# Stores of the weight forms' high parts issued by ScalarE instead of SyncE, in a fused attention and two-MLP kernel

## The chip, the cores and the metric

The kernel runs as one program on one core of a Trainium2 chip. The metric is the device time of one execution in microseconds (us). Engines are named as in the profile: PE (TensorE), DVE (VectorE), ACT (ScalarE), POOL (GpSimd) and SP (SyncE, which here does nothing but issue transfers).

## What is computed

Attention over 4 x 8 heads of 576 positions with a mask by blocks of 64, then two MLPs without bias on the 2304 rows that come out of it, all in 32-bit floats:

```python
scores = scale * np.matmul(q, k.transpose(0, 1, 3, 2))
scores = np.where(mask, scores, -1000000000.0)
attn = np.exp(scores - np.max(scores, axis=-1, keepdims=True))
attn = attn / (np.sum(attn, axis=-1, keepdims=True) + 1e-09)
x = np.matmul(attn, v)              # 2304 x 512 after the heads are joined
h = x @ w_in                        # 512 -> 2048
x = (h * np.clip(h + 3.0, 0.0, 6.0) / 6.0) @ w_out
h = x @ w2_in
out = (h * np.tanh(softplus(h))) @ w2_out
```

## The kernel before

**Matmuls in three products.** Each 32-bit operand is kept as a high and a low part (`wh`, `wl`; `Xh`, `Xl`; `gh`, `gl`); a product is high x high, high x low and low x high (`products`, L840 to L847). A high part is an ACT copy that rounds (`copy`, L313, recorded at L316), the low part a subtraction on DVE or POOL (`sub`, L320, recorded at L322).

**Stages.** Attention runs to about 165 us. The first MLP follows in three blocks of tokens (512, 256, 512): for each of 16 slices of the inner dimension `in1` makes `h` in one of two PSUM banks (12 matmuls), ACT computes `e` = relu(h + 3), DVE multiplies (`multiply`, L950), ACT copies `gh`, DVE subtracts `gl`, and two slices later `out1` multiplies with them (12 matmuls). The last 1024 tokens (`in3`, `out3`, from 388 us) and the whole second MLP (from about 535 us) take block products in seven forms instead of eight. That needs sums of blocks of the weights:

- `unit1(q)`, L1232 to L1273, eight times: sums of blocks of the first `w_out`, high and low parts stored to the DRAM tensor `w1d`;
- `unit2(u)`, L1004 to L1046, sixteen times: two raw tiles of 512 KB are loaded (L1012), rebased from 64-bit floats by ACT, POOL and DVE (`rebase`, L849), four block sums `S` formed, and for four pieces the high part is copied by ACT (`hx`, `Sh`; L1043) and stored (L1044), the low part subtracted (`q`, `ex`; L1045) and stored (L1046), all to `w2d`. All units use the same tiles, so a piece can be written again only when its store has landed, and a raw tile loaded again only when it was read.

The units run beside the matmuls, from about 237 us (`unit1`) and 287 us (`unit2`) to 533 us. `weights1` and `weights2` load the forms back.

**Order.** Nothing is ordered by hand there. `Schedule` (L123 to L248) takes every operation with its engine, a cost and, for transfers, a time to land, plays the whole program once, and issues each engine's list in the order of the start times that come out. TensorE's operations are bound to the order of the program; the others are chosen by how soon TensorE needs what follows from them. A transfer is an operation of SP whose cost grows with its size, so SP's list is the planner's picture of all DMA:

```python
"POOL": (145, 2.156), "POOL_ONE": (100, 0.99), "POOL_V": (260, 0.87), "SP": (100, 3.05),
```

(first number fixed, second per KB for SP: 880 for 256 KB, in the planner's units). At run time each engine takes its list strictly in order.

Of the kernel before, what the change touches and what calls it, by code (L numbers as in the profile page):

```python
# [55 lines left out]
LANDS = 6000  # L56
# [41 lines left out]
class Ref:  # L98
# [14 lines left out]
    @staticmethod  # L113
    def real(*views):
        def one(x):
            if isinstance(x, Ref):
                return x.get()
            return [one(y) for y in x] if isinstance(x, (list, tuple)) else x

        return [one(x) for x in views]  # L120
# [130 lines left out]
def f32(ap):  # L251
    return ap.bitcast(F32)
# [7 lines left out]
def fused_kernel(ctx: ExitStack, tc: tile.TileContext, qT, kT, vv, w1, w2, outT):  # L260
    nc = tc.nc
# [18 lines left out]
    w1d = dpool.tile([NQ, 2, P, 1792], F32, tag="w1d", name="w1d")  # L280
    w2d = dpool.tile([NQ, 2, 2, P, 1792], F32, tag="w2d", name="w2d")
# [18 lines left out]
    plan = Schedule()  # L300
    real = Ref.real
# [4 lines left out]
    def dma(kb, reads, writes, dst, src, **kw):  # L306
        def run(e):
            d, s = real(dst, src)
            nc.sync.dma_start(d, s)

        return plan.add(one("SP", "SP", kb), reads, writes, run, land=kw.pop("land", 2500), **kw)

    def copy(n, reads, writes, dst, src, func=AF.Copy, psum=False, after=(), **kw):  # L313
        def run(e):
            d, s = real(dst, src)
            nc.scalar.activation(d, s, func, **kw)  # L316

        return plan.add(one("ACT", "ACT_PSUM" if psum else "ACT", n), reads, writes, run, after=after)

    def sub(engines, reads, writes, dst, a, b, **kw):  # L320
        return plan.add(
            engines, reads, writes, lambda e: ENG[e].tensor_sub(*real(dst, a, b)), **kw)  # L322
# [78 lines left out]
    def load_v(p):  # L401
        dma(90, [], [("v", p % 2)], at["v", p % 2], vv[p], land=LAND, behind=tuple(begun[-4:]))
# [346 lines left out]
    for n in range(2):  # L749
        for j in range(2):  # L750
            r, c = slice(64 * j, 64 * j + 64), slice(64 - 64 * j, P - 64 * j)
# [16 lines left out]
    for g in range(NG + LAG_V + NU):  # L768
        p, i = divmod(g, NU)
        if g < NG:  # L770
# [7 lines left out]
            if g in EARLY_ROUNDS:  # L778
                f, c = divmod(EARLY_ROUNDS.index(g), 2)
# [3 lines left out]
        u, i = divmod(g - LAG_R, NU)  # L783
        if i == 0 and 0 <= u < NP:
            sums(u)
        u, i = divmod(g - LAG_V, NU)
# [187 lines left out]
    def before(n):  # L974
        return [*plan.readers.get(n, ()), *[x for x in [plan.writer.get(n)] if x is not None]]
# [28 lines left out]
    def unit2(u):  # L1004

        q, c = u // 2, u % 2
        at = [("r", 0), ("val", 1)]
        vs = [buf[x] for x in at]
        dst = w2d[q, c].rearrange("t p (s c) -> t p s c", c=256)
        for i in range(2):  # L1010
            raw = buf["raw", i]
            dma(512, [], [("raw", i)], raw.rearrange("p n t -> p (n t)"),  # L1012
                w2[2 * q + i, :, 512 * c:512 * c + 512].bitcast(U32), after=odd if u == 0 else (), land=LANDW)
            rebase(
                raw, buf["r", i], buf["val", i], (("raw", i), ("r", i), ("val", i), ("val", i)),
                buf["val", i] if i else None)
        cc, ch = buf["S"], buf["Sh"]
        a11, a12, a21, a22 = vs[0][:, 0:256], vs[0][:, 256:512], vs[1][:, 0:256], vs[1][:, 256:512]
        psum = lambda n: one("DVE", "DVE_PSUM", n)

        pool = lambda n: one("POOL", "POOL", n)

        def sums(n, a, b, reads, of, add=False):
            plan.add(
                of, reads, [("S", n)],
                lambda e: (ENG[e].tensor_add if add else ENG[e].tensor_sub)(*real(cc[:, n], a, b)))

        sums(0, a21, a22, [at[1]], pool(256), True)
        sums(3, a11, a21, at, psum(256))
        sums(1, cc[:, 0], a11, [at[0], ("S", 0)], psum(256))  # L1030
        sums(2, a12, cc[:, 1], [at[0], ("S", 1)], psum(256))
        view = lambda t: t.rearrange("p (s c) -> p s c", c=256)
        lo = [view(buf["q", n]) for n in range(2)]
        parts = (
            (512, view(buf["hx", 0]), view(vs[0]), ("hx", 0), [at[0]], slice(0, 2), lo[0], [("q", 0)]),
            (256, view(buf["hx", 1][:, 0:256])[:, 0:1], view(vs[1])[:, 1:2], ("hx", 1), [at[1]], slice(6, 7),
             lo[1][:, 0:1], [("q", 1)]),
            (512, ch[:, 0:2], cc[:, 0:2], ("Sh", 0), [("S", 0), ("S", 1)], slice(2, 4), view(buf["ex", 0]), [("ex", 0)]),
            (512, ch[:, 2:4], cc[:, 2:4], ("Sh", 1), [("S", 2), ("S", 3)], slice(4, 6), view(buf["ex", 1]), [("ex", 1)]),
        )  # L1040
        for i, (n, x, v, xn, vn, cs, to, tn) in enumerate(parts):
            of = (either(n) if i > 1 else pool(n)) if i else psum(n)
            copy(n, vn, [xn], x.bitcast(F32R), v, psum=not i)  # L1043
            dma(n // 2, [xn], [("w2d", q, c, 0, i)], dst[0][:, cs], x, land=LANDS if u < 2 else 2500)  # L1044
            sub(of, vn + [xn], tn, to.bitcast(F32R), v, x)  # L1045
            dma(n // 2, tn, [("w2d", q, c, 1, i)], dst[1][:, cs], to, land=LANDS if u < 2 else 2500)  # L1046

# [184 lines left out]
    def unit1(q):  # L1232

        f, g = 2 * q, 2 * q + 1
        names = lambda f: [("wt", f, 1, h) for h in range(2)]
        for h in range(2):
            dma(128, [("wt", f, 1, h)], [("w1d", q, h, 0)], w1d[q, h, :, 0:256], f32(half_b(f, h)[:, 0:256]))
            dma(256, [("wt", g, 1, h)], [("w1d", q, h, 3)], w1d[q, h, :, 1280:1792], f32(half_b(g, h)))
        m = q % 2
        v, u, vn, un = buf["val", m], buf["r", m], ("val", m), ("r", m)  # L1240
        a11, a12, a21, a22 = u[:, 0:256], u[:, 256:512], v[:, 0:256], v[:, 256:512]
        cc, ch = [raw_f32(i).rearrange("p (s c) -> p s c", c=256) for i in range(2)] if m else [buf["S"], buf["Sh"]]
        S, Sh = [("S", m, i) if m else ("S", i) for i in range(4)], [("Sh", m, i) if m else ("Sh", i) for i in range(2)]
        first = len(plan.ops)
        old = [k for i in range(2) for k in plan.readers.get(("raw", i), ())] if q == 1 else []

        def add(engines, reads, writes, dst, a, b, after=()):
            plan.add(
                engines, reads, writes, lambda e: ENG[e].tensor_add(*real(dst, a, b)), after=[*old, *after])

        psum, pool = one("DVE", "DVE_PSUM", 256), one("POOL", "POOL", 256)
        for i, x in enumerate((f, g)):
            cs, hl = slice(256 * i, 256 * i + 256), [f32(half_b(x, h)) for h in range(2)]
            ui, vi = un + (i,), vn + (i,)
            copy(256, names(x), [ui], u[:, cs], hl[0][:, 0:256], after=before(un))
            add(psum, names(x) + [ui], [ui], u[:, cs], u[:, cs], hl[1][:, 0:256])
            add(pool, names(x), [vi], v[:, cs], hl[0][:, 256:512], hl[1][:, 256:512], before(vn))
        un, vn = [un, un + (0,), un + (1,)], [vn, vn + (0,), vn + (1,)]
        add(pool, vn, [S[0]], cc[:, 0], a21, a22)
        sub(psum, un + vn, [S[3]], cc[:, 3], a11, a21, after=old)  # L1260
        sub(psum, un + [S[0]], [S[1]], cc[:, 1], cc[:, 0], a11)
        sub(psum, un + [S[1]], [S[2]], cc[:, 2], a12, cc[:, 1])
        for i in range(2):
            n, cs = [S[2 * i], S[2 * i + 1]], slice(2 * i, 2 * i + 2)
            to = [w1d[q, h, :, 256 + 512 * i:768 + 512 * i].rearrange("p (s c) -> p s c", c=256) for h in range(2)]
            copy(512, n, [Sh[i]], ch[:, cs].bitcast(F32R), cc[:, cs])
            dma(256, [Sh[i]], [("w1d", q, 0, 1 + i)], to[0], ch[:, cs])
            ln = ("ex" if m else "q", i)
            lo = buf[ln].rearrange("p (s c) -> p s c", c=256)
            sub(one("POOL", "POOL", 512), n + [Sh[i]], [ln], lo.bitcast(F32R), cc[:, cs], ch[:, cs])  # L1270
            dma(256, [ln], [("w1d", q, 1, 1 + i)], to[1], lo)
        if m:
            odd.extend(range(first, len(plan.ops)))  # L1273
# [169 lines left out]
    for kind, s, *i in sequence():  # L1443
# [50 lines left out]
        i, = i  # L1494
        q, p = s % NQ, s // NQ
# [99 lines left out]
```

## Time and profile before

| | us |
|---|---|
| median of 3 runs (lowest, highest) | 909.99 (909.47, 910.26) |
| the profiled execution | 908.69 |
| its span, first to last instruction | 906.8 |
| TensorE's matmuls | 899.3 (99%) |
| DVE, ACT, POOL busy | 699.2, 561.1, 713.5 |
| DMA queue, share of 16 engines | 76.6% |

The span is what the trace shows; the 1.9 us between it and the execution's time lie around it. All transfers run in one hardware queue, q1, begun by SP. Busy time of matmuls is modelled at their ends, and issuing a transfer does not count as busy time.

### The profile page before, as it was taken

To read this page: it belongs to the slowest core of one execution; us is meant where nothing else is said; L and a number is where in the kernel's file an instruction comes from. 1 tells how busy PE (TensorE), PEld (TensorE's weight loads), DVE (VectorE), ACT (ScalarE), POOL (GpSimd) and SP (SyncE) were. 2 spreads that over 40 slices of the span, in tenths; PEclk is the share of its full clock that TensorE was granted. 3 is DMA by queue.
4 is the path that set the end of the run, shared out by engine and by line. 5 is a ranking of instruction groups with operands and counts; after the bars stand their busy time and mean duration, and the time that the engine had idled before them with its cause. 6 is when DMAs were issued, how large, how long until landed. Compare 5 with 4: busy or idle time off the path is not lost.

```text
span 906.8 us, 16469 instructions
## 1 busy us (share of the span) xinstructions
PE 899.3 (99%) x5297; PEld 825.3 (91%) x5297; DVE 699.2 (77%) x1244; ACT 561.1 (62%) x1279; POOL 713.5 (79%) x722
## 2 busy tenths in 40 slices
PE   8999999999999999999999999999999999999998
PEld 7999999888899888878888889999999999999998
DVE  6999988888744756779999999687677666766657
ACT  7999999866754635465565666445554445545452
POOL 8998898578997535877877868788897978967775
PEclk9999999999999999999999999999999999999999
DMA  6887784496776799986987998886788867787752
GB/s 179 273 249 233 232 275 138 160 402 228 239 240 230 250 339 312 313 301 194 293 290 253 308 312 302 295 324 241 258 287 319 301 244 275 242 319 245 255 216 85
DMA packets 114918, 236.90 MB, mean 261 GB/s; under 512 B 23856, under 2 KB 37776, under 8 KB 114832
## 3 DMA queue, kind: packets, MB, share of 16 engines
q1 hardware_dynamic: 114832, 235.86, 76.6%
q8 instruction: 42, 0.69, 0.3%
q14 instruction: 44, 0.36, 0.1%
HBM read 169.87 MB, written 62.99 MB: 257 GB/s over the span
## 4 chain that ended last, share of the span: by engine, by line
PE 92%; DVE 2%; POOL 2%; DMA 2%; issue 1%; ACT 1%; SPq 0%; DVEq 0%; ACTq 0%; POOLq 0%
PE y L845 12%; PE y L846 12%; PE y L847 12%; PE h L845 10%; PE h L846 10%; PE h L847 10%; PE o L670 6%; PE t L606 5%; PE r L846 3%; PE r L847 3%; PE r L845 3%; PE s L565 3%; PE s L525 2%; DMA w2d<-ex 1%; DVE nm L507 1%
## 5 line engine op out<-in xcount | busy, mean ns | idle before, releaser
L845 PE MATMUL y<-X,wh 128*128 128x384 f32 (+1 forms) x448 | 156.0, 348 | 0.2 <-issue 0.2
L847 PE MATMUL y<-X,wl 128*128 128x384 f32 (+1 forms) x448 | 155.9, 348 | 0.0
L846 PE MATMUL y<-X,wh 128*128 128x384 f32 (+1 forms) x448 | 155.9, 348 | 0.0
L846 PE MATMUL h<-wl,wh 128*128 128x384 f32 (+1 forms) x320 | 114.0, 356 | 0.0
L847 PE MATMUL h<-wh,wl 128*128 128x384 f32 (+1 forms) x320 | 114.0, 356 | 0.0
L845 PE MATMUL h<-wh,wh 128*128 128x384 f32 (+1 forms) x312 | 111.1, 356 | 0.9 <-DVE xr L952 0.9
L322 POOL TENSOR_TENSOR X<-e,X 128x384 fp32r<-128x384 f32 (+1 forms) x90 | 99.3, 1110 | 13.3 <-ACT X L316 12.1
L1199 DVE TENSOR_TENSOR sgh<-y,sgh 128x384 f32<-128x384 f32 x129 | 70.0, 555 | 31.1 <-PE y L847 30.8
L845 PEld LDWEIGHTS y<-X,wh 128*128 128x128 f32 x448 | 84.1, 188 | 5.0 <-issue 0.5
L847 PEld LDWEIGHTS y<-X,wl 128*128 128x128 f32 x448 | 84.1, 188 | 4.3
L846 PEld LDWEIGHTS y<-X,wh 128*128 128x128 f32 x448 | 84.1, 188 | 4.2
L316 ACT ACTIVATE X<-e 128x384 fp32r<-128x384 f32 (+1 forms) x96 | 52.7, 551 | 52.2 <-POOL e L322 48.4
L322 POOL TENSOR_TENSOR X<-xr,X 128x384 fp32r<-128x384 f32 (+2 forms) x40 | 44.5, 1112 | 48.0 <-ACT X L316 40.0
L322 DVE TENSOR_TENSOR z<-t,z 128x512 fp32r<-128x512 f32 (+1 forms) x112 | 67.6, 629 | 8.9 <-ACT z L316 7.9
L845 PE MATMUL h<-X,wh 128*128 128x512 f32 (+1 forms) x192 | 68.4, 356 | 0.0
L846 PE MATMUL h<-X,wh 128*128 128x512 f32 (+1 forms) x192 | 68.0, 354 | 0.0
L847 PE MATMUL h<-X,wl 128*128 128x512 f32 (+1 forms) x192 | 68.0, 354 | 0.0
L846 PE MATMUL y<-gl,wh 128*128 128x512 f32 (+1 forms) x192 | 67.9, 354 | 0.0
L845 PE MATMUL y<-gh,wh 128*128 128x512 f32 (+1 forms) x192 | 67.9, 354 | 0.0
L847 PE MATMUL y<-gh,wl 128*128 128x512 f32 (+1 forms) x192 | 67.9, 354 | 0.0
L670 PE MATMUL o<-z,vh 128*128 128x320 f32 (+4 forms) x416 | 64.1, 291 | 0.7 <-DVE z L322 0.6
L846 PEld LDWEIGHTS h<-wl,wh 128*128 128x128 f32 x320 | 60.1, 188 | 5.1
(227 smaller groups left out, 2630.4 us busy)
## 6 DMA issues: line engine op xcount, KB each, us to landing
raw<-w SPq DMA_DIRECT2D x64, 512.0 KB
wh<-w2d SPq DMA_DIRECT2D x48, 512.0 KB
wl<-w2d SPq DMA_DIRECT2D x48, 512.0 KB
wh<-w2d SPq DMA_DIRECT2D x48, 384.0 KB
wl<-w2d SPq DMA_DIRECT2D x48, 384.0 KB
x1d<-x SPq DMA_DIRECT2D x32, 288.0 KB
w2d<-Sh SPq DMA_DIRECT2D x32, 256.0 KB
w2d<-ex SPq DMA_DIRECT2D x32, 256.0 KB
```

Source lines behind the costliest of these rows:

```text
L316: nc.scalar.activation(d, s, func, **kw)
L322: engines, reads, writes, lambda e: ENG[e].tensor_sub(*real(dst, a, b)), **kw)
L507: lambda e: nc.vector.tensor_reduce(to, view, axis=AX.X, op=ALU.max, negate=True))
L525: nc.tensor.matmul(sc[:, a:z], stationary[i][:, x, :], ks[:, y, a - o:z - o], start=k == 0 and a in (0, 512), stop=k == 2, skip_group_chec ...
L565: nc.tensor.matmul(part(h)[:, a:a + w], qs[r, x, QUERY_AT[i]:QUERY_AT[i] + P], ks[r, y, 0:w], start=False, stop=k == 2, skip_group_check=True)
L606: nc.tensor.transpose(tp[:, c, :], x, ident)
L670: nc.tensor.matmul(out, vb[:, c, h].rearrange("p t d -> p (t d)"), mov, start=k == 0, stop=k == len(todo) - 1, skip_group_check=True)
L845: nc.tensor.matmul(b, wh, xh, start=start and k == 0, stop=False, skip_group_check=True)
L846: nc.tensor.matmul(b, wh, xl, start=False, stop=False, skip_group_check=True)
L847: nc.tensor.matmul(b, wl, xh, start=False, stop=last, skip_group_check=True)
L1199: nc.vector.tensor_add(dst, src, old)
```

## The change

A new helper records a transfer as an operation of ACT with a fixed cost of 400 and a landing time of 5000, and issues it from ACT's own queue. It takes the place of `dma` for the high stores of `unit2` (all four pieces, 64 stores in all) and for the two stores of high sums in `unit1` (16 stores). The low stores stay on SP.

```diff
+    def dma_beside(reads, writes, dst, src, land=5000):
+
+        def run(e):
+            d, s = real(dst, src)
+            nc.scalar.dma_start(d, s)
+
+        return plan.add((("ACT", 400, False),), reads, writes, run, land=land)
...
             copy(n, vn, [xn], x.bitcast(F32R), v, psum=not i)
-            dma(n // 2, [xn], [("w2d", q, c, 0, i)], dst[0][:, cs], x, land=LANDS if u < 2 else 2500)
+            dma_beside([xn], [("w2d", q, c, 0, i)], dst[0][:, cs], x)
             sub(of, vn + [xn], tn, to.bitcast(F32R), v, x)
...
             copy(512, n, [Sh[i]], ch[:, cs].bitcast(F32R), cc[:, cs])
-            dma(256, [Sh[i]], [("w1d", q, 0, 1 + i)], to[0], ch[:, cs])
+            dma_beside([Sh[i]], [("w1d", q, 0, 1 + i)], to[0], ch[:, cs])
```

Since the planner plays the program anew, the lists of ACT, DVE, POOL and SP all change from about 237 us on; TensorE's list is the same. Lines behind L312 stand 8 further down in the changed kernel. Two places matter below.

ACT, around the activation of the last slice before `in3` (`e2<-h1`, the sixteenth slice of the third block). `r<-raw` begins the rebase of a raw tile, `hx` and `Sh` are high parts, `o` the results of `out1`, `wh0_12` to `wh0_14` the token tiles for `in3`, `xr1<-h0` the first activation of `in3`. Before:

```order
L316 ACTIVATE wh0_12_3083<-xr1_163 128x512
L316 ACTIVATE hx1_165<-val1_159 128x256
L316 ACTIVATE e2_2503<-h1_2498 128x512
L316 ACTIVATE hx0_162<-r0_2499 128x512
L316 ACTIVATE gh2_2506<-h1_2498 128x512
L316 ACTIVATE wh0_13_3132<-xr0_160 128x512
L316 ACTIVATE Sh_167<-S_166 128x512 x2
L316 ACTIVATE r1_2500<-raw1_158 128x512
```

And in the changed kernel:

```order
L324 ACTIVATE wh0_12_3083<-xr1_163 128x512
L324 ACTIVATE r1_2500<-raw1_158 128x512
L324 ACTIVATE e2_2503<-h1_2498 128x512
L324 ACTIVATE Sh_167<-S_166 128x512
L324 ACTIVATE gh2_2506<-h1_2498 128x512
L324 ACTIVATE Sh_167<-S_166 128x512
L317 DMA w2d_80<-Sh_167 128x512
L324 ACTIVATE r0_2499<-raw0_156 128x512
L317 DMA w2d_80<-Sh_167 128x512
L324 ACTIVATE hx1_165<-val1_159 128x256
L317 DMA w2d_80<-hx1_165 128x256
```

The copy of a raw tile now stands right ahead of `e2<-h1`. It is the ninth of `raw1`, and eight of `raw0` stand ahead of it; before, seven of each stood ahead of `e2<-h1`, and the eighth of `raw1` came behind it. Three stores follow.

SP, around the stores of the third block's results (`x2d<-o`), which follow the last `out1`. Before:

```order
L309 DMA w2d_80<-Sh_167 128x512
L309 DMA x2d_78<-o0_2684 128x512
L309 DMA x2d_78<-o1_2685 128x512
L309 DMA w2d_80<-Sh_167 128x512
L309 DMA w2d_80<-ex0_2692 128x512
L309 DMA raw1_158<-w2 128x1024
L309 DMA w2d_80<-ex1_2693 128x512
L309 DMA w2d_80<-hx1_165 128x256
```

And in the changed kernel:

```order
L309 DMA raw1_158<-w2 128x1024
L309 DMA o2_2686<-rsd_77 64x512 x2
L309 DMA w2d_80<-ex1_2693 128x512
L309 DMA raw0_156<-w2 128x1024
L309 DMA xr0_160<-x1d_76 128x512
L309 DMA w2d_80<-q0_161 128x512
L309 DMA xr1_163<-x1d_76 128x512
L309 DMA w2d_80<-q1_164 128x256
L309 DMA w2d_80<-ex0_2692 128x512
L309 DMA raw1_158<-w2 128x1024
L309 DMA w2d_80<-ex1_2693 128x512
L309 DMA x2d_78<-o0_2684 128x512
```

The stores of `hx` and `Sh` are gone from the list. The first row is the ninth load of `raw1`, the tenth stands ahead of `x2d<-o0`; before, the ninth stood behind it.

## Rows read from the trace of the kernel before

**Rows 1.** The head and first part of the page: span, busy time.
```profile
span 906.8 us, 16469 instructions
...
PE 899.3 (99%) x5297; PEld 825.3 (91%) x5297; DVE 699.2 (77%) x1244; ACT 561.1 (62%) x1279; POOL 713.5 (79%) x722
```
**Rows 2.** Waits of PE from 230 us on: us in total, times, longest.
```profile
PE h L845 <- DVE xr L952: 0.9, 1, 0.9
PE y L845 <- issue: 0.2, 1, 0.2
```
**Rows 3.** Stretches: length, each engine's busy us (instructions), granted clock, DMA share, GB/s.
```profile
core 0: us, PE busy (x) PEld busy (x) DVE busy (x) ACT busy (x) POOL busy (x), PEclk, DMA share, GB/s
260.00:280.00 20.00, 20.00 (x169) 20.00 (x168) 12.14 (x31) 11.15 (x28) 19.59 (x21) 1.00 0.74 262
287.00:300.00 13.00, 13.00 (x104) 12.66 (x103) 6.66 (x14) 5.36 (x14) 4.99 (x6) 1.00 0.54 177
320.00:340.00 20.00, 20.00 (x90) 16.58 (x89) 11.02 (x18) 8.80 (x17) 5.51 (x7) 1.00 1.00 351
300.00:388.00 88.00, 88.00 (x401) 73.36 (x400) 57.20 (x91) 45.09 (x84) 53.15 (x52) 1.00 0.94 317
440.00:460.00 20.00, 20.00 (x90) 16.55 (x89) 19.57 (x34) 12.51 (x23) 16.92 (x18) 1.00 0.89 293
```
**Rows 4.** Timeline of PE, 385 to 395 us: start, us, instruction, idle before it.
```profile
385.41 0.39 PE L845 MATMUL y<-gh,wh 128*128 128x512 f32 x1
...
385.64 0.39 PE L846 MATMUL y<-gl,wh 128*128 128x512 f32 x1
...
388.13 0.39 PE L845 MATMUL h<-wh,wh 128*128 128x512 f32 x1
...
394.61 0.50 PE L845 MATMUL h<-wh,wh 128*128 128x512 f32 x1 [0.88 <-DVE xr L952]
```
**Rows 5.** Timeline of ACT, 321 to 394 us.
```profile
321.29 0.64 ACT L316 ACTIVATE r<-raw 128x512 f32<-128x512 f32 x1 [0.30 <-DMA raw<-w]
...
380.76 0.58 ACT L316 ACTIVATE e<-h 128x512 f32<-128x512 f32 x1
...
383.97 0.60 ACT L316 ACTIVATE gh<-h 128x512 fp32r<-128x512 f32 x1
...
392.93 0.42 ACT L316 ACTIVATE hx<-val 128x256 fp32r<-128x256 f32 x1 [1.93 <-DMA w2d<-ex]
393.25 0.58 ACT L316 ACTIVATE xr<-h 128x512 f32<-128x512 f32 x1
```
**Rows 6.** Timeline of DVE, 383 to 394 us.
```profile
383.25 0.69 DVE L952 SCALAR_TENSOR_TENSOR h<-e,h 128x512 f32<-128x512 f32 x1
...
384.66 0.68 DVE L322 TENSOR_TENSOR gl<-h,gh 128x512 fp32r<-128x512 f32 x1
...
393.87 0.69 DVE L952 SCALAR_TENSOR_TENSOR xr<-xr,h 128x512 f32<-128x512 f32 x1 [1.02 <-ACT xr L316]
```
**Rows 7.** Issues of the moved stores on SP: ns shortest/median/longest, first and last start.
```profile
L309 SPq DMA_DIRECT2D w2d<-hx x32: 319/379/817, 298.3 to 527.8; - x32
...
L309 SPq DMA_DIRECT2D w2d<-Sh x32: 319/383/1047, 302.5 to 529.2; - x32
```
**Rows 8.** Issue list: count and KB each.
```profile
raw<-w SPq DMA_DIRECT2D x64, 512.0 KB
...
w2d<-Sh SPq DMA_DIRECT2D x32, 256.0 KB
```
**Rows 9.** Timeline of SP, raw loads.
```profile
287.17 0.90 SPq L309 DMA_DIRECT2D raw<-w  x2
...
297.28 0.33 SPq L309 DMA_DIRECT2D raw<-w  x1
...
314.85 0.33 SPq L309 DMA_DIRECT2D raw<-w  x1
```
**Rows 10.** Chain that ended last, 366 to 386 us: start, us, what.
```profile
369.33 7.18 DMA w2d<-ex
```

## Prediction, before the changed kernel was run

> **What bounds the kernel now.** Start with the page's first part: TensorE is busy 899.3 us of a span of 906.8 [rows 1]. The diff leaves TensorE's instructions and their order untouched, so the time can only change by the 7.5 us in which TensorE does nothing. The list of waits says where they are [rows 2]: after the attention, which the change does not reach, one wait of 0.9 us and one of 0.2 us are left; the rest lies at the start and behind the last matmul. So the change can win about 1 us. What it can lose has no such limit: any instruction of another engine that comes late enough stops TensorE, and the question is which one comes close.
>
> The table of stretches answers the next question, how full everything else is [rows 3]. From 300 to 388 us, where the first half of the weight forms is made beside the first layer's second half, DMA is 0.94 busy and moves 317 GB/s, while ScalarE works 45 of 88 us. There DMA is the scarce thing. From 440 to 460 us it is VectorE, 19.57 of 20 us.
>
> Then the place where TensorE is nearest to waiting: the change from `out1` to `in3` at 388 us. The last `out1` starts at 385.41, and its second matmul, 0.23 us later, reads `gl` [rows 4]. ScalarE's `e<-h` for it began at 380.76, `gh` at 383.97 [rows 5], VectorE's `h` at 383.25 and `gl` at 384.66 for 0.68, so `gl` was done at 385.34 [rows 6]: about 0.3 us to spare. Eight microseconds later ScalarE stood 1.93 us before an `hx` copy, so that `xr<-h` began only at 393.25; VectorE's multiplication waited for it, and TensorE stopped 0.88 us at 394.61 [rows 4 to 6]. ScalarE takes its work in order: what one copy waits for, the activation behind it waits for too.
>
> **The change, part by part.** *Issue.* 80 stores leave SP: 64 of `w2d` (32 of `hx`, 32 of `Sh`) and 16 of `w1d`. One issue took SP 0.32 to 0.38 us [rows 7], so ScalarE takes on some 80 x 0.38 = 30 us between 237 and 530 us, about a tenth of that stretch. In the stretches of rows 3 it is busy 0.41 to 0.63 of the time, and its work for TensorE waits for nothing else, so I cost this at nothing by itself; without that cover it would be 0.4 us per store that stands ahead of an activation. No row shows a store begun by ScalarE: from below the price is nothing (it would run beside the activations), from above SP's longest, 1.05 us; I take 0.38, SP's median for the same kind of transfer. The 16 `w1d` stores fall where DMA is 0.74 busy and ScalarE works 11.15 of 20 us [rows 3]: nothing.
>
> *Work given to another engine.* VectorE gets two more `ex` subtractions and GpSimd two fewer, beside single ones that change the other way. At 0.69 us each that is 1.4 us in VectorE's stretch of nearly no gaps; TensorE had no wait there, so nothing, with 1.4 us kept for the upper end.
>
> *The order of loads.* This is the large term. SP's list no longer carries the high stores, so the planner lets the raw loads and low stores move up. The bytes are the same, but more of them are now wanted earlier. Count up to the activation that the last `out1` needs, `e2<-h1` (the order above): before, ScalarE has taken seven raw tiles of each kind by then; now nine `raw1` and eight `raw0`, and the ninth `raw1` stands right ahead of `e2`. From the first raw load on, SP issues up to that ninth load 17 raw loads (8.5 MiB), 27 low stores (5.88), 12 of `x1d` (3.0), 12 of `rsd` (1.5), 16 of `w1d` (3.5), 4 of `x2d` and 2 stores to `w1d` (0.5 each): 23.38 MiB by the issue list and the order's shapes [rows 8]. ScalarE has by then issued 8 + 14 stores of 256 KB and 8 of 128 KB, 6.5 MiB. Together 29.88 MiB = 31.33 MB.
>
> When can they have moved? From 287 to 300 us DMA moved 13 x 0.177 = 2.30 MB; the first raw loads were issued at 287.17, and the next had to wait until the first were read, so I leave this as it is. From 300 us I let DMA be always busy. Its rate at full share is 317/0.94 = 337 GB/s [rows 3]. The remaining 29.03 MB need 86.1 us: the load lands at 386.1. Then `r` (0.64), `e`, `h`, `gh` and `gl` (0.58 + 0.69 + 0.60 + 0.68 and some 0.1 between them) [rows 5, 6] end at 389.4, where TensorE wants `gl` at 385.6. **TensorE waits 3.8 us.** The bounds: at 351 GB/s, the best stretch of this mix [rows 3], the load lands at 382.7 and the wait is 0.4; at the 317 actually reached it lands at 391.6 and the wait is 9.3. I take 337, the mean of the very stretch with its gaps closed, because the raw loads now stand further ahead and keep the queue filled.
>
> The same sum for the activations before it gives loads that land some 1 to 4 us behind their place, but those activations have more to spare (10.9 us from a finished `h` to its `out1`, four groups of twelve matmuls of 2.72 us as the last one's [rows 4], for a chain of 2.7), so nothing. That a landing in this stretch does take long is seen twice: a raw load issued at 314.85 held ScalarE's copy until 321.29 [rows 5, 9], and one `ex` store took 7.18 us [rows 10].
>
> *The old wait.* With TensorE 3.8 us later, the list behind `e2` (two `Sh`, three stores, `r0`, `hx1`, three `o`, two `wh`) has time to run before `in3` needs `h0` again, so the 0.9 us go.
>
> Sum: 3.8 - 0.9 = +2.9 us. Against the profiled execution, 908.69, that is 911.6; that execution lies 1.3 us below the median of the three runs, 909.99, so the forecast for a median is **912.9**. By the bounds: 0.4 - 0.9 = -0.5 gives 909.5, and 9.3 - 0.9 = +8.4 gives 918.4.
>
> From 391 us on the raw loads have room again: DMA is 0.89 busy [rows 3] and by ScalarE's list the units, now one ahead, end seven activations from `h` earlier. Nothing waits for that end.
>
> **The rivals.** *The load still comes in time (not slower).* Place: the same `r1` copy ahead of `e2`. If DMA reaches 353 GB/s from 300 us on, the ninth load lands by 382.3 and nothing waits; the 0.9 us may go as well, since the high stores no longer stand behind raw loads in SP's queue and `hx` is free sooner: 909.99 - 0.9 = 909.1. For it: 351 GB/s stood for 20 us at share 1.00 [rows 3], and a first part of the loads may move before 300 us. Against it: the stretch's own rate at full share is 337.
>
> *Only the issue moves.* What would follow if the loads were held by something else than SP's place in line, such as the buffers they fill: then they are issued when they were before, and the time stays 909.99. For it: SP waited for others' work in between, since the second pair of raw loads came 10 us behind the first [rows 9]. Against it: the new list asks for two tiles more by the same activation, and ScalarE cannot pass them. The Trainium skill ("DMA: Bandwidth & Descriptors", "Issuing engines are not separate DMA queues") says that transfers started by several engines run on the same 16 DMA engines and that starting them from several saves only the time of issue. By that rule alone the sum is zero; it also speaks against any gain in rate. That DMA is 0.94 busy from one queue agrees with it; no run here shows two queues yet.
>
> *ScalarE itself comes late (slower).* Place: 400 to 530 us, where VectorE has no gaps [rows 3] and each activation of `in3` feeds it. Some 28 stores stand there; if every third one holds an activation by 0.38 us and VectorE cannot make it up, that is 28/3 x 0.38 = 3.5 us less 0.9: 912.6. It decides when a store is issued while TensorE's bank is waiting. Against it: no wait of TensorE there before, and ScalarE works 12.51 of 20 us.
>
> **How the numbers follow.** A measurement of this kernel can tell about 0.2%, 1.8 us, from no change. Forecast 0.52, of which 0.03 fall under 1.8 us; in time 0.30; only the issue moves 0.07; ScalarE late 0.11. Slower by over 0.2%: 0.49 + 0.11 = 0.60. Within 0.2%: 0.03 + 0.27 + 0.07 = 0.37. Faster: 0.03, since TensorE has only 1.1 us of waits to give and the rest is chance between runs. The range reaches from the first rival, 909.1, to 917.5, just short of the upper bound: it leaves out about one in ten at each end. The forecast's own range is 909.5 to 918.4.
>
> **What would show it.** In the profile after: still no change in TensorE's instructions; `w2d<-Sh` and `w2d<-hx` issued by ACT for about 0.38 us; a share of DMA above 0.96 from 300 to 388 us and more GB/s than 317; ScalarE's `r<-raw` copies released by `raw<-w` by several us in sum before 390; one wait of TensorE of 2 to 5 us for `gl` or `gh` at `y` (or for `xr` at `h`) between 380 and 400 us, and the old 0.88 gone. I am wrong if TensorE has no new wait there, if the waits lie behind 400 us or have ScalarE's stores ahead of them, or if DMA's share from 300 to 388 us stays at 0.94.

## The result, and the profile after

The changed kernel takes **919.48 us** (median of 4 runs, 919.05 to 922.05), against 909.85 for the kernel before on the same chip: a ratio of 1.0106, with a 95% interval of 1.0092 to 1.012. It is 9.6 us slower. 912.9 was forecast, with 917.5 as the upper end of the range: the sign was right, the size was not.

First the head of the page after, its waits of TensorE from 230 us on (us in total, times, longest), and its stretches (length, busy us and instructions of each engine, granted clock, DMA share, GB/s):

```profile
span 917.7 us, 16477 instructions
...
PE 903.8 (98%) x5297; PEld 826.5 (90%) x5297; DVE 698.4 (76%) x1247; ACT 561.8 (61%) x1279; POOL 709.2 (77%) x719
```
```profile
PE h L853 <- DVE gl L330: 5.3, 4, 2.4
PE y L853 <- ACT gh L324: 1.2, 1, 1.2
PE h L853 <- DVE e L330: 0.7, 1, 0.7
PE h L853 <- DVE xs L960: 0.4, 1, 0.4
PE y L854 <- DVE gl L330: 0.2, 1, 0.2
PE h L853 <- DVE xr L960: 0.2, 1, 0.2
```
```profile
260.00:280.00 20.00, 20.00 (x169) 20.00 (x168) 11.28 (x30) 10.71 (x27) 18.92 (x20) 1.00 0.73 262
320.00:340.00 20.00, 20.00 (x90) 16.57 (x89) 10.44 (x18) 6.50 (x12) 5.18 (x6) 1.00 0.92 308
340.00:360.00 20.00, 14.95 (x64) 11.36 (x63) 13.44 (x23) 9.43 (x19) 5.90 (x8) 1.00 0.97 333
...
300.00:388.00 88.00, 82.71 (x372) 67.43 (x371) 58.95 (x96) 42.65 (x79) 42.73 (x44) 1.00 0.96 321
440.00:460.00 20.00, 20.00 (x90) 16.54 (x89) 19.40 (x35) 13.44 (x23) 15.56 (x16) 1.00 0.90 303
```

TensorE has as many instructions as before [rows 1] and the clock is full. The old wait for `xr` went from 0.9 to 0.2 us [rows 2]. New is a wait of 5.3 us in four pieces that has no counterpart: `in1` waits for `gl`. It lies where TensorE did not wait at all before: from 340 to 360 us it now works 14.95 of 20 us. VectorE's full stretch, 440 to 460 us, still costs nothing [rows 3].

Since TensorE's order is the same in both kernels, each of its instructions has a twin. The start of an instruction in the changed kernel less the start of its twin before, along the timeline of TensorE, says where the 10.9 us between the two spans were lost. At the time before of 170, 330, 370, 410 and 600 us the distance is 1.18, 1.18, 7.79, 10.44 and 10.86 us. So 6.6 us were lost between 330 and 370, 2.65 between 370 and 410, and 0.4 behind that. The 1.18 us arise in the attention; two profiles below in which no store moved show 1.2 us there too, so they are not the change's.

The timeline of TensorE after has these pauses (in brackets the idle time and what ended it):

```profile
342.93 0.50 PE L853 MATMUL h<-X,wh 128*128 128x512 f32 x1 [2.42 <-DVE gl L330]
...
349.87 0.50 PE L853 MATMUL h<-X,wh 128*128 128x512 f32 x1 [1.19 <-DVE gl L330]
...
357.05 0.50 PE L853 MATMUL h<-X,wh 128*128 128x512 f32 x1 [1.45 <-DVE gl L330]
...
368.55 0.50 PE L853 MATMUL h<-X,wh 128*128 128x512 f32 x1 [0.24 <-DVE gl L330]
...
394.53 0.50 PE L853 MATMUL y<-gh,wh 128*128 128x512 f32 x1 [1.16 <-ACT gh L324]
395.26 0.50 PE L854 MATMUL y<-gl,wh 128*128 128x512 f32 x1 [0.22 <-DVE gl L330]
```

The first pause, followed back on the timeline of ScalarE (ACTq rows are the issues of the moved stores), then of SyncE, then in SyncE's waits from 322 to 332 us, then in the chain of work that ended last:

```profile
323.27 0.35 ACTq L317 DMA_DIRECT2D w2d<-hx  x1
...
326.94 0.33 ACTq L317 DMA_DIRECT2D w2d<-Sh  x1
327.32 0.60 ACT L324 ACTIVATE gh<-h 128x512 fp32r<-128x512 f32 x1 [1.90 <-DMA raw<-w]
...
332.72 0.60 ACT L324 ACTIVATE gh<-h 128x512 fp32r<-128x512 f32 x1 [0.76 <-DVE h L960]
337.04 0.63 ACT L324 ACTIVATE r<-raw 128x512 f32<-128x512 f32 x1 [3.73 <-DMA raw<-w]
339.70 0.60 ACT L324 ACTIVATE hx<-r 128x512 fp32r<-128x512 f32 x1 [2.03 <-DVE S L1034]
340.19 0.59 ACT L324 ACTIVATE e<-h 128x512 f32<-128x512 f32 x1
```
```profile
320.28 0.33 SPq L309 DMA_DIRECT2D raw<-w  x1
320.71 0.41 SPq L309 DMA_DIRECT2D o<-x1d  x1
...
322.29 0.40 SPq L309 DMA_DIRECT2D wh<-w1d  x1
323.22 4.77 SPq L309 DMA_DIRECT2D o<-rsd  x2
329.74 0.33 SPq L309 DMA_DIRECT2D wl<-w1d  x1
330.15 1.09 SPq L309 DMA_DIRECT2D o<-rsd  x2
331.35 0.53 SPq L309 DMA_DIRECT2D raw<-w  x1
```
```profile
SPq L309 <- DMA o<-x1d: 3.8, 1, 3.8
SPq L309 <- DMA w2d<-hx: 1.7, 1, 1.7
```
```profile
323.27 6.40 DMA w2d<-hx
...
331.35 5.67 DMA raw<-w
```

Read it backwards. TensorE's last `in1` matmul into this bank began at 331.96, so the bank was full at about 332.2, and ScalarE was free at 333.3. The activation `e<-h` started at 340.19. In between ScalarE, which takes its list in order, stood 3.73 us before a raw tile and 2.03 us before an `hx` copy that VectorE makes ready from that tile. The raw tile was late because its load was issued only at 331.35, 11 us behind the one before it, and took 5.67 us to land. SyncE had not issued it earlier because of two waits for landings ahead of it in its list: 3.8 us at an `o<-rsd` load, until a token load of its own (`o<-x1d`, begun at 320.71) had landed, and 1.7 us at `wl<-w1d`, until a store that *ScalarE* had begun at 323.27 had landed 6.40 us later, at 329.67. So most of this standing is for SyncE's own slow landings, and ScalarE's store is the end of it. In the same order with SyncE issuing (next section) this load was issued at 327.38, and TensorE's first pause was 0.48 us.

Why should a weight load wait for a store with which it shares no data? The compiled program's rows say it. In this program each transfer that SyncE or ScalarE starts is given one of eight semaphores (DMAHW0 to DMAHW7) in turn, in the order of the program, both lists counted together, and first waits until the transfer eight places before it, which had the same one, has landed. Four rows of SyncE's list after, and one of ScalarE's:

```
310 L309 DMA wh_1_2069<-w1d 128x512 [waits DMAHW7_49,PE_49]
...
313 L309 DMA wl_1_2070<-w1d 128x512 [waits DMAHW4_49,PE_49]
...
315 L309 DMA o_2686<-rsd 64x512 [waits DMAHW6_49]
316 L309 DMA raw_156<-w 128x1024 [waits DMAHW7_49,DVE_49,Activation_49]
```
```
539 L317 DMA w2d<-hx_162 128x512 [waits DMAHW4_49,Activation_49]
```

Place 4 was that store's. The trace agrees: its records name one of eight semaphores for each of the 792 transfers, 99 on each, and no transfer begins before the one ahead of it on the same semaphore has landed. The raw load itself had place 7 behind a weight load of SyncE's own, which landed at 330.64, so without ScalarE's store it could have begun at most 0.7 us sooner at this point. So the two lists are tied: SyncE waits for ScalarE's stores to land, and ScalarE, with all its activations behind the store, for SyncE's loads (before the `gh` at 327.32 ScalarE was idle for 1.90 us; its `h` was ready at 326.15, but the store at 326.94, ahead of it, waited until 326.87 for a raw load that neither of them reads). SyncE's waits for landings between 300 and 420 us add up to 26.9 us in the changed kernel; in the kernel before they were 8.0, and in the run of the next section with the change's order and SyncE issuing 7.5. So the 26.9 go with ScalarE's issue and not with the order.

### The profile page after: what moved, and what is told of

It is laid out like the page before. It is cut to its first block, busy times and chain, and to the rows that moved or that the text cites. A ratio compares the mean times of both kernels' runs of the same rounds, so it can differ in the third digit from the quotient of the medians.

```text
span 917.7 us, 16477 instructions
## 1 busy us (share of the span) xinstructions
PE 903.8 (98%) x5297; PEld 826.5 (90%) x5297; DVE 698.4 (76%) x1247; ACT 561.8 (61%) x1279; POOL 709.2 (77%) x719
## 4 chain that ended last, share of the span: by engine, by line
PE 53%; DMA 6%; DVE 3%; POOL 2%; ACT 1%; issue 1%; SPq 0%; ACTq 0%; POOLq 0%; DVEq 0%
PE y L853 9%; PE y L854 9%; PE y L855 9%; PE h L854 6%; PE h L853 6%; PE h L855 6%; PE r L854 3%; PE r L853 3%; PE r L855 3%; DMA w2d<-hx 2%; DMA raw<-w 2%; DVE r L747 1%; DMA w2d<-ex 1%; DMA o<-x1d 1%; POOL xr L1004 1%
## 5 line engine op out<-in xcount | busy, mean ns | idle before, releaser
L330 POOL TENSOR_TENSOR X<-e,X 128x384 fp32r<-128x384 f32 (+1 forms) x88 | 96.3, 1102 | 13.9 <-ACT X L324 12.7
L853 PEld LDWEIGHTS h<-wh,wh 128*128 128x128 f32 x312 | 58.5, 188 | 7.4 <-DVE e L330 1.1
```

What stands on the lines that cost most here:

```text
L853: nc.tensor.matmul(b, wh, xh, start=start and k == 0, stop=False, skip_group_check=True)
```

## The experiments

Two theories were set up after this reading, and a third beside them. **Order:** without the stores' SyncE time in its costs, the planner starts units earlier, and the lists ask for more bytes before 390 us than the DMA engines move; who issues does not matter. **Places:** the eight places, held across two in-order lists, cost time whatever the order. **Issue time:** 0.33 us of ScalarE per store. Kernels before gave 909.6 to 909.7 us beside each group of runs.

*One part at a time.* The change's order, with SyncE issuing:

```
 def dma_beside(reads, writes, dst, src, land=5000):
...
-            nc.scalar.dma_start(d, s)
+            nc.sync.dma_start(d, s)
```


> The changed kernel's plan and order, but the 80 stores issued by SP at the same places of the program. Theory A (the early loads: the new order asks for more bytes by each activation than DMA moves, whoever issues them): as slow as the changed kernel, ratio to before 1.008 to 1.012, TensorE's waits between 335 and 415 us still there. Theory B (shared places: every transfer waits at its issue until the one eight places ahead of it in the program has landed, and with stores on ACT that wait stands in ACT's list ahead of activations, while SP waits for ACT's stores): at least half of the loss goes, 1.000 to 1.005. Theory C (issue time of 0.33 us per store on ACT): the loss goes, 1.000 to 1.003.

Measured: 917.08 us, ratio 1.0083 (1.0066 to 1.01), in the range of *order*. The order alone makes 7.4 of the 9.6 us; that ScalarE issues adds 2.4 (919.48 less 917.08). The two intervals overlap a little, the single runs do not (at most 917.35 here, at least 919.05 there).

The old order (the stores keep their old cost in the plan), with ScalarE issuing:

```
-            dma(n // 2, [xn], [("w2d", q, c, 0, i)], dst[0][:, cs], x, land=LANDS if u < 2 else 2500)
+            dma(n // 2, [xn], [("w2d", q, c, 0, i)], dst[0][:, cs], x, issue=nc.scalar, land=LANDS if u < 2 else 2500)
```


> The plan and order of the kernel before, but the 80 stores issued by ACT at their places of the program. Theory A: no change, 0.999 to 1.002, since the loads stand where they stood. Theory B: slower, 1.004 to 1.012, ACT waiting ahead of stores for landings. Theory C: 1.001 to 1.004, ACT's activations late by 0.33 us here and there.

Measured: 911.77 us, 1.0025 (1.0015 to 1.0035), so 2.1 us for the same move. Two ways to isolate it agree. By the ranges set ahead this value falls to *issue time* (1.001 to 1.004) and below *places* (1.004 to 1.012); two runs further down, with copies in place of the issues and with fewer bytes, tell them apart. One place in ScalarE's timeline of this kernel:

```profile
336.43 1.55 ACTq L309 DMA_DIRECT2D w2d<-hx  x2
338.03 0.63 ACT L316 ACTIVATE r<-raw 128x512 f32<-128x512 f32 x1 [3.08 <-DMA w2d<-Sh]
```

The copy `r` reads a raw tile, and `w2d<-Sh` carries nothing of it. It stood behind two `hx` stores, and each of these waited until the transfer eight places before it had landed. TensorE lost nothing there, so how the 2.1 us come about is not shown wait by wait. What the profile shows is that SyncE's waits for landings from 300 to 420 us rose here too, from 8.0 to 18.1 us, and that in the same order DMA moved 305 GB/s from 300 to 340 us instead of 321; in the change's order it is 307 against 325. The stretch in the kernel before, in this one, in the change's order with SyncE issuing, and in the change:

```profile
300.00:340.00 40.00, 40.00 (x189) 33.61 (x188) 23.81 (x40) 19.63 (x38) 18.27 (x19) 1.00 0.94 321
```
```profile
300.00:340.00 40.00, 40.00 (x190) 33.54 (x189) 23.99 (x42) 17.15 (x32) 17.89 (x20) 1.00 0.92 305
```
```profile
300.00:340.00 40.00, 39.65 (x187) 32.94 (x185) 24.74 (x41) 18.84 (x36) 17.11 (x19) 1.00 0.97 325
```
```profile
300.00:340.00 40.00, 40.00 (x189) 33.57 (x188) 23.54 (x40) 17.32 (x33) 15.61 (x17) 1.00 0.93 307
```

The likely reading is that two lists that wait for each other leave the DMA engines emptier: their share falls from 0.94 to 0.92 and from 0.97 to 0.93.

The change, with a blank SyncE step of the old cost beside each moved store in the plan:

```
+        plan.add(one("SP", "SP", kb), reads, [], lambda e: None)
         return plan.add((("ACT", 400, False),), reads, writes, run, land=land)
```


> The change, and in the planner beside each store on ACT a blank operation of SP with the cost that the store had there, so that SP's loads are planned with DMA's time taken up as before; the stores are issued by ACT. Theory A: the loss goes, 0.999 to 1.003. Theory B: most of it stays, 1.004 to 1.012. Theory C: 1.001 to 1.004.

Measured: 914.74 us, 1.0059 (1.0039 to 1.0078). The total falls in the range of *places* (1.004 to 1.012), yet the distance to before says otherwise: nothing is lost between 330 and 410 us (0.43 at 330, -0.09 at 410), although ScalarE issues the stores and the helper's cost of 400 and landing time of 5000 stayed in the plan. So the SyncE time taken out of the plan was the cause there. The profiled execution is the fastest of the four (913.22 us; the slowest took 917.04); what the others lost beyond it is not shown. In the profiled one 4.0 us are lost in another place, between 540 and 600. There the plan gave VectorE a subtraction that GpSimd makes in the kernel before. The timeline of GpSimd, then of VectorE:

```profile
545.69 1.30 POOL L331 TENSOR_TENSOR X<-e,X 128x512 fp32r<-128x512 f32 x1
546.94 1.03 POOL L1164 TENSOR_TENSOR wl<-Sh,wh 128x384 fp32r<-128x384 f32 x1
547.91 1.30 POOL L331 TENSOR_TENSOR X<-e,X 128x512 fp32r<-128x512 f32 x1
549.16 1.02 POOL L1164 TENSOR_TENSOR wl<-S,wh 128x384 fp32r<-128x384 f32 x1
550.13 1.03 POOL L331 TENSOR_TENSOR hx<-Sh,val 128x384 f32<-128x384 f32 x1
```
```profile
546.63 5.08 DVE L331 TENSOR_TENSOR X<-e,X 128x512 fp32r<-128x512 f32 x1
```

Beside GpSimd's unbroken row of operations VectorE needed 5.08 us for a subtraction that took it 0.68 to 1.35 us elsewhere, and ended 0.55 us behind that row. The run with the units held back, below, repeats it. What in the row holds it up is not shown: in the kernel before GpSimd works through as unbroken a row from 536.85 to 556 us, and no VectorE subtraction beside it took more than 1.29 us.

Only the 64 stores of the second layer moved, and only the 16 of the first:

```
-            dma_beside([Sh[i]], [("w1d", q, 0, 1 + i)], to[0], ch[:, cs])
+            dma(256, [Sh[i]], [("w1d", q, 0, 1 + i)], to[0], ch[:, cs])
```


> The change for the 64 stores to w2d alone; the 16 to w1d stay on SP. All theories: nearly the whole loss, 1.007 to 1.012, since TensorE's new waits begin behind 335 us; if the 16 stores matter, below 1.006.


```
-            dma_beside([xn], [("w2d", q, c, 0, i)], dst[0][:, cs], x)
+            dma(n // 2, [xn], [("w2d", q, c, 0, i)], dst[0][:, cs], x, land=LANDS if u < 2 else 2500)
```


> Only the 16 stores of the first layer's forms (w1d, between 237 and 300 us) move to ScalarE's queue; the 64 of the second layer's stay on SyncE's with their old cost in the plan. The run with only the 64 moved took 916.62 us, 2.9 less than the whole change. If the two parts add: 912 to 913.3. If the 16 cost only together with the 64: 909.3 to 910.5.

Measured: 916.62 us (1.0059 to 1.0089) for the 64, 909.33 us (0.9993 to 1.0011) for the 16. The loss is the 64's; the 16 cost nothing alone, and 2.9 us on top of the 64, though the plan made anew for each of the two also gives another order.

*Bytes.* A first attempt halved the weight loads from the third group on:

```
+            w = (cs.stop - cs.start) // (2 if s > 1 else 1)
...
-                f32(dst), w1d[s, h, :, cs], after=[last_out[3]] if piece == 3 and s < 2 else (),
+                f32(dst)[:, 0:w], w1d[s, h, :, cs.start:cs.start + w], after=[last_out[3]] if piece == 3 and s < 2 else (),
```


> The change's order with all stores on SyncE's queue (917.08 us when it ran), but each load of the first layer's weight forms from the third group on carries half of its bytes: as many transfers, in the same order, some 5 MB less between 320 and 400 us; those halves keep old data, so the output is not the reference's. Theory 'bytes' (the DMA engines are full between 300 and 390 us, so landings take 6 us and more, and unit work planned earlier waits for them with the activations behind it): the loss between 335 and 420 us falls from 7.5 us to 2 or less, so 909.5 to 912. Theory 'order of the lists' (the unit's steps stand ahead of the activations however fast the transfers are): 915 or more. Theory 'eight places' (a transfer waits until the one eight before it has landed): between them, 911 to 915, since shorter transfers free places sooner too.

Measured: 918.16 us (1.0076 to 1.0106). It missed its aim: those groups load behind 400 us. The page shows 5.5 MB less in all, but 329 GB/s from 340 to 360 us (336 without the edit), and the loss from 330 to 410 stayed at 7.2 us. It is a control: bytes taken away behind 400 us bring nothing. The second attempt takes them where the loss is:

```
-            dma(w * 5 // 32 + 10, made, [dst], to,
-                x1d[k, n, :, :, t0:t0 + w].rearrange("d h n -> (d h) n"), land=land)
+            part = w if t0 < T1 else w // 2
+            dma(w * 5 // 32 + 10, made, [dst], to[:, 0:part],
+                x1d[k, n, :, :, t0:t0 + part].rearrange("d h n -> (d h) n"), land=land)
```
(and so for the `rsd` loads and all groups of weight loads)

> The change's order with all stores on SyncE's queue (917.08 us when it ran), but all loads of the first layer's weight forms and the token and scale loads from token 1280 on carry half of their bytes: as many transfers, in the same order, some 5 MB of the 33 MB between 300 and 400 us less, none of them of the second layer's units. The halves not loaded keep old data, so the output is not the reference's. Theory 'bytes' (the DMA engines are full there, so landings take 6 us and more): the loss between 335 and 420 us falls from 7.5 us to 2.5 or less, 909.5 to 912.5. Theory 'order of the lists' (the units' steps stand ahead of the activations whatever the transfers take): 915 or more.

> The same as the run with fewer bytes beside the units, but the 80 stores issued by ScalarE as in the change (which took 919.48 us, 2.4 more than the same order on SyncE). Theory 'eight places' (ScalarE's list waits for landings that SyncE's transfers owe): with emptier DMA engines landings are shorter, so less than 1 us above the run before it. Theory 'issue time on ScalarE': 2 to 3 us above it, as with all bytes.

Measured: 913.26 us (1.0024 to 1.005) with SyncE issuing, 911.57 us (1.0014 to 1.0034) with ScalarE. 300 to 388 us in the first, then in the second:

```profile
300.00:388.00 88.00, 87.11 (x393) 71.41 (x391) 61.80 (x101) 45.85 (x86) 49.35 (x51) 1.00 0.89 292
```
```profile
300.00:388.00 88.00, 86.92 (x391) 71.12 (x389) 61.50 (x102) 46.27 (x86) 49.61 (x51) 1.00 0.91 296
```

With the same order, the same count of transfers and a DMA share of 0.89 to 0.91 instead of 0.96 to 0.97, what is lost from 330 to 370 us falls from 4.3 to 1.2 us and, with ScalarE issuing, from 6.6 to 0.3. What is lost from 370 to 410 falls little, from 3.1 to 2.1, and not at all (2.65 and 2.8). So bytes explain the larger part. The first run missed its range by 0.8 us: 2 to 3 us stay lost around the last `out1`. They may belong to the order as such, with a raw tile ahead of the activation, but that is not shown, since profiles of kernels in the old order lose 1.4 to 2.7 us there too (table below). And ScalarE's issue no longer costs anything that can be told from the spread: the run is 1.7 us below SyncE's, with intervals that overlap, where it was 2.4 above with full engines. An issue takes its 0.33 us in both, so its time alone does not explain the 2.4; that emptier engines also leave more slack to hide it is not excluded.

*Units held back.* The change's order with SyncE issuing, each raw load charged double in the plan:

```
-            dma(512, [], [("raw", i)], raw.rearrange("p n t -> p (n t)"),
+            dma(1024, [], [("raw", i)], raw.rearrange("p n t -> p (n t)"),
```


> The same order with all stores on SyncE's queue, but the plan charges each raw load of the second layer's units twice its SyncE time (1.56 us more, so 3.1 us for a unit, what its four stores of upper bits were charged before), so that the plan begins units as far apart as before the change. Theory 'order of loads' (units begun sooner want more bytes between 320 and 400 us than the DMA engines move): the loss is gone, 909.5 to 912. If what counts is the place of the stores in the lists and not when the units begin: 915 to 917.

Measured: 913.77 us (1.0028 to 1.0057), between the two. Again the distance tells more than the total: -0.15 us at 330 and at 370, 2.5 at 410, 6.8 at 600. The loss from 330 to 370 is gone, as the theory has it; the last 4.2 us stand where the same subtraction on VectorE is slow again (5.15 us in this profile).

*Places, and issue time.* More transfers for the same bytes, in the change's order with SyncE issuing and in the kernel before:

```
-            dma(n // 2, tn, [("w2d", q, c, 1, i)], dst[1][:, cs], to, land=LANDS if u < 2 else 2500)
+            dma_halves(n // 2, tn, [("w2d", q, c, 1, i)], dst[1][:, cs], to, land=LANDS if u < 2 else 2500)
```


> The same order with all stores on SyncE's queue, each 128x512 store of the second layer's lower bits as two transfers of half the bytes: 48 more transfers, the same bytes in packets of the same size. Theory 'bytes': 916.4 to 917.8, as without the split. Theory 'eight places': with eight transfers in flight carrying fewer bytes, SyncE waits for landings more often and loads start later: 919 or more.

> The control to the run with halves: the kernel before, each 128x512 store of the second layer's lower bits as two transfers of half the bytes (48 more transfers, same bytes, same order). If a transfer costs because it takes one of eight places while the DMA engines are nearly full, before pays too, but less, since its order leaves more slack: 910 to 912.5. If a transfer costs only SyncE's issue time: 909.3 to 910.2.

Measured: 920.29 us (1.0099 to 1.013), 3.2 more than without halves; and 909.97 us (0.9991 to 1.0011), no difference. So 48 more transfers cost nothing in themselves. In the crowded order they do: SyncE's waits for landings from 300 to 420 us double, from 7.5 to 15.1 us, where in the kernel before they go from 8.0 to 7.2. The halves do not move in packets of the same size, as was expected, but in packets of 1 KB instead of 2 KB. From 300 to 388 us a packet of 1 KB took 46 ns and one of 2 KB 91 to 94, so the DMA engines' time for the same bytes stayed nearly the same.

The kernel before, with a small ScalarE copy in place of each issue:

```
             nc.sync.dma_start(d, s)
+            if beside is not None:
+                nc.scalar.activation(real(idle)[0], real(beside)[0][:, 0, 0:128], AF.Copy)
```


> The kernel before, with all stores on SyncE's queue, and beside each of the 80 stores a small ScalarE copy of 128 columns into a spare tile (about 0.3 us, as long as an issue), at the place in ScalarE's list at which the issue stood when the old plan's stores were issued by ScalarE (911.77 us). Theory 'issue time on ScalarE': 911 to 912.5, as that run. Theory 'eight places' (ScalarE's list waits for landings of SyncE's transfers): 909.3 to 910.4, as before.

Measured: 910.31 us (0.9999 to 1.0019): 0.7 us more, which is within what the interval leaves for no change, where the issue itself cost 2.1. The copies took 0.30 us each, an issue 0.33. The intervals of the two overlap a little, so a share of ScalarE's time is not excluded; the run with fewer bytes speaks against it.

The distance to the kernel before, gained in each stretch of its time (us, from the profiled execution of each):

| kernel | up to 330 | 330 to 370 | 370 to 410 | 410 to 600 |
|---|---|---|---|---|
| the change | 1.18 | 6.61 | 2.65 | 0.42 |
| its order, SyncE issues | 0.32 | 4.32 | 3.14 | 0.42 |
| old order, ScalarE issues | 1.73 | -0.01 | 2.68 | -0.03 |
| SyncE's time kept in the plan | 0.43 | -0.01 | -0.51 | 4.03 |
| only the 16 stores to `w1d` moved | 0.94 | 0.00 | 1.54 | 0.10 |
| raw loads held back | -0.15 | 0.00 | 2.68 | 4.24 |
| low stores in halves | 0.20 | 5.00 | 4.10 | 0.42 |
| fewer bytes, SyncE issues | 0.80 | 1.17 | 2.08 | 0.43 |
| fewer bytes, ScalarE issues | 0.15 | 0.34 | 2.78 | 0.42 |
| before, low stores in halves | 1.82 | -0.01 | 0.18 | -0.01 |
| before, ScalarE copies | 1.16 | -0.01 | 1.43 | 0.36 |

Between 370 and 410 us small losses show in many of them, also where the median is that of before; this is the place at which before already paused 0.88 us [rows 4], and single executions differ there by a microsecond or two: with only the 16 stores moved, at a median of 909.33, the profiled execution took 911.23 us and lost 1.54 there. No kernel tried beats the kernel before by more than the spread: TensorE has only about 1 us of waits to give.

## Why the prediction was wrong

*What bounds the kernel* held: TensorE's instructions did not change, and nearly all that was lost lies at waits of TensorE for other engines' work.

*Issue.* The stores took ScalarE 326 to 327 ns at the median, below the 0.38 taken:

```profile
L317 ACTq DMA_DIRECT2D w2d<-hx x32: 326/327/500, 297.0 to 518.4; - x32
L317 ACTq DMA_DIRECT2D w2d<-Sh x32: 326/326/362, 300.6 to 521.4; - x32
```

As time on ScalarE this is nearly free, as costed. But "I cost this at nothing by itself" failed: the issue cost 2.1 us with the old order and 2.4 with the new one. As far as the runs tell, that is not the 0.33 us of each but the wait for a place that an issue brings into ScalarE's list, and the place that it holds against SyncE. For the rule of the Trainium skill ("DMA: Bandwidth & Descriptors", "Issuing engines are not separate DMA queues") the trace agrees that a second issuing engine brings no rate: from 300 to 340 us it took 5% off (307 against 325 GB/s). That only the time of issue changes is not so here (2.1 and 2.4 us more).

*The order of loads* was the right mechanism, and its first step is right in the plainest way. The 17th raw load, forecast to land at 386.1 us, was issued at 385.29 and let ScalarE go on at 390.96:

```profile
388.04 0.60 ACT L324 ACTIVATE gh<-h 128x512 fp32r<-128x512 f32 x1
...
390.96 0.63 ACT L324 ACTIVATE r<-raw 128x512 f32<-128x512 f32 x1 [0.71 <-DMA raw<-w]
391.52 0.57 ACT L324 ACTIVATE e<-h 128x512 f32<-128x512 f32 x1
...
393.88 0.60 ACT L324 ACTIVATE gh<-h 128x512 fp32r<-128x512 f32 x1
```

The step that failed is "I take 337, the mean of the very stretch with its gaps closed". The gaps did not close: 321 GB/s at a share of 0.96. With 321 the same 29.03 MB land at 390.4, and the same sum gives a wait of 8.1 us; TensorE lost 9.3 between 330 and 410. The run with SyncE issuing fits as well: 325 GB/s give 389.3 and 7.0 us; measured were 388.4 and 7.5. So the term of 3.8 us was 9.3, the very value of its upper bound, at the 317 GB/s that before reached. That rate, with its own gaps, was the better guess.

That the corrected sum comes so close is partly luck. Between 287 and 300 us 2.94 MB moved (226 GB/s), where the sum has 2.30. The chain from `r` to the `y` that reads `gl` took 4.3 us (390.96 to 395.26) and not 3.3, since an `Sh` copy stood between `e2` and `gh2`, as the order above shows, and waited for VectorE. And TensorE wanted `gl` 1.18 us later than the sum says, the time lost in the attention. At that `y` TensorE was 8.4 us behind the kernel before (395.26 less 385.64 less 1.18); the rest of the 9.3 arose behind it.

*Where it falls* was wrong too. "Those activations have more to spare (10.9 us ...), so nothing": the pauses at 342.93, 349.87 and 357.05 us are just there. I counted up to the `out1` that reads `gl`. But TensorE's next `in1` into the same bank has to wait until `gl` has read the bank, and it comes one group of matmuls earlier. The `in1` of the first pause has this twin in the kernel before:

```profile
339.17 0.39 PE L845 MATMUL h<-X,wh 128*128 128x512 f32 x1
```

So it was due at 340.35 (339.17 and the 1.18 of the attention); less 332.2 that is 8.2 us, of which the chain takes 2.7. ScalarE was busy 1.1 us more, so 4.4 were to spare, and the first late tile held `e` by 6.9. So the lateness of the loads was paid in pieces as it grew, from 343 us on, and only 1.4 us (1.16 + 0.22) were left for the last `out1`, where I had put all of it.

*The old wait* went, from 0.9 to 0.2 us, as forecast. *Work given to another engine* cost nothing in the stretch that the prediction meant, 440 to 460 us.

Of the rivals, "the load still comes in time" falls with the rate. "Only the issue moves" falls with the run in the change's order on SyncE, since the order makes three quarters of the loss. "ScalarE itself comes late" had its place behind 400 us; there the loss is 0.4 us. Of the signs named, the share of DMA came out at 0.96, just at the value named, and ScalarE's waits for raw tiles at 4.4 us in sum before 400; the wait of 2 to 5 us between 380 and 400 was 1.4. A sign of being wrong was met in part: stores of ScalarE do stand in the chain ahead of the first pause.

What stays open: by which waits the 2.1 and 2.4 us of ScalarE's issue reach TensorE, and whether the 370 to 410 us loss of the single profiles is more than their scatter. Full engines and the eight places were not separated further: a place is held for as long as its transfer takes to land, so fewer bytes relieve both.

## What to carry to other kernels

Moving the start of a transfer to another engine moves more than its 0.3 us: it moves the wait before it into that engine's in-order list, so look up what each issue waits for (its data, and the places in flight) before costing it at the time of issue. Where a planner's costs stand in for a shared resource, taking work off one engine's account lets it order more of that resource than there is; keep the bytes on the account even if another engine issues them (the run that did so lost nothing from 330 to 410 us, but its new plan lost time elsewhere). When a sum of bytes decides, start from the rate that the stretch reached with its gaps, and test the slack of each activation against the next writer of its bank, not against its reader alone.

## What the runs showed of the hardware that was not expected

Transfers that the two engines start share eight places in this program, in program order, so a weight load of SyncE stood 1.7 us until a store of ScalarE that had nothing to do with it had landed, 6.40 us after its start. A second issuing engine went with a lower rate from 300 to 340 us, in one and the same order: 305 GB/s instead of 321, and 307 instead of 325. With fewer bytes it did not (303 with ScalarE, 295 with SyncE). Split in halves, 48 stores cost 3.2 us in a crowded stretch and nothing in the kernel before. One VectorE subtraction of 128x512 took 5.08 and 5.15 us, in two kernels, instead of 0.68 to 1.35 while GpSimd worked through a row of tensor operations without a gap; why only this one did is not shown.
